# A gated MLP block: the token mix by one step of Strassen's algorithm, with its first pair of tiles inside the stage before

## The chip, the cores and the metric

The kernel runs on one core of a Trainium2 chip. A core has five engines that run side by side and meet at semaphores: TensorE (PE, matrix products; its weight loads are listed as PEld), VectorE (DVE), ScalarE (ACT), GpSimd (POOL) and SyncE (SP, which here issues transfers). Matrix products land in PSUM, a small memory of eight banks; the rest lives in SBUF, with 128 partitions. The metric is the device time of one execution in microseconds.

## What is computed

A block with adaptive layer norm: first a long convolution with gates (part A), then a gated MLP whose gate mixes the tokens (part B). The change touches part B only, with S = 2048 tokens, D = 640 and Fh = 864:

```python
h = _layernorm(x, axis=-1) * (1 + cb) + sb
z = _gelu(einsum('bsd,df->bsf', h, w_in))        # 2048 x 1728
z1 = z[..., :Fh]
z2 = _layernorm(z[..., Fh:], axis=-1)
g = einsum('ts,bsf->btf', w_sp, z2) + b_sp[None, :, None]   # the token mix
out = x + gb * einsum('bsf,fd->bsd', z1 * g, w_out)
```

The token mix multiplies a 2048 x 2048 matrix with a 2048 x 864 one. The result is bf16.

## The kernel before

Tokens are handled in 16 tiles of 128; four tiles make a group (TB = 4), so there are four groups, 0 to 3. The features of one half of z are cut into two pieces of 432 columns (FC), which fit one PSUM bank each.

**The plan.** Everything up to the normalised z2 is a list of some thousand small operations, each with an engine and its dependencies (`Plan.op`). They are issued in an order that is written out in the text `ORDER`: `P1020` means operation 1020 on PE, and A, D, G and S stand for ACT, DVE, POOL and SP. Each engine works its own operations strictly in this order.

**The z stage** (`z_group`, one call per group) is the plan's last part. For each tile, DVE adds statistics (`ln2`, L696), which are combined (L821); POOL takes the inverse root (`rstd2`, L184 and L185), DVE makes a product of it (L825), and one of DVE, ACT and POOL normalises the tile (`zx`, L835 to L839). The normalised group is transposed: group 0 on PE with its modulation on DVE and ACT (L850, L861, L863), in two halves of two tiles (`hfl`, `hmod`); groups 1 to 3 by a DMA transpose on SP (`turn`, L881), after which five modulations (`hmod2`, L887 and L889) follow on DVE, ACT or POOL. Then PE makes 16 products per group (`zz`, issued through a helper at L237), each with five matmuls of 432 columns: eight for the second half of z (which becomes z2) and eight for the first half (z1). ACT applies gelu to each (L912). For z2, DVE then takes statistics (`stz`, L918), combines them (L922), POOL and DVE make scale and shift (`rstdz`, `nmrz`), and DVE or ACT normalises z2 in place (`zn`, L933 and L935). The products go through four PSUM banks, two with the tag `pu` and two with `pz`; a product needs a bank that an earlier gelu has read. Some extra matmuls (`fill`) keep PE busy in an earlier stage.

**The token mix** follows the plan, in plain program order (the functions below). At its start SP loads transposed tiles of w_sp by DMA transpose (`load_w`, five ahead, L967) and w_o (seven DMAs). For each token tile t, `mix(t)` runs, for each of two column pieces, 16 matmuls (L974) over all token tiles of z2 in one PSUM bank, and DVE adds the bias and multiplies by z1 (L977) into the buffer u. A DMA transpose on SP turns u into uT (L980); the last tile is turned by PE and ACT (`turn_last`, L986 and L987). Two tiles later `project(t)` runs two times seven matmuls with w_o (L995), DVE adds x (L997), and the tile is written out. At t = 1 DVE multiplies w_o by the gate gb (seven products, L1013).

Memory: the tiles of part A live in pools that are closed when the plan has run; w_sp, w_o, u and uT come to lie where they were.

Of the kernel before, what the change touches and what calls it, by code (L numbers as in the profile page):

```python
# [69 lines left out]
D729 D759 P735 P749 P589 A590 D758 D731 D732 G692 D690 G760 D761 D691 A762 G763 P1036 P1037 P764 D736 D733 P765 D771  # L70
D766 D767 D768 D734 D772 P742 G667 D693 D750 G773 D774 G775 D737 D740 D739 G610 D741 D738 D694 A769 S756 A770 P787
D637 P784 D696 A788 A776 S757 D695 D836 P818 G669 P791 A785 A792 P777 D835 D837 P778 D834 A782 A819 D779 D643 D780
D781 P816 A817 G838 D839 D840 D841 A783 P794 A795 P814 P820 A842 A821 D843 S844 G848 D697 D699 G845 A815 D702 D751
D753 D701 D712 D743 D700 D698 D744 D748 D903 P798 A799 P812 A813 P826 A827 D747 P805 A806 P808 P801 A809 P822 D703
D752 D642 D849 D754 A846 A847 D704 A802 P824 A825 P886 A823 D640 A887 P850 A851 D706 P853 D611 G644 A854 D641 P857
D745 A858 P884 D900 P874 D902 A885 D746 D901 G904 D905 A875 D906 D755 D909 D907 D800 P890 A891 P880 A881 P882 P892
G908 S910 A893 A883 D876 D705 P888 A889 G912 A911 P860 P871 D810 A872 D803 D646 D807 D967 P878 A861 A913 P864 D647
A865 P867 A879 A868 D915 D914 P958 D648 D969 P923 P916 A924 A917 P946 D786 A959 P944 D645 A947 D966 D968 G970 D971
D972 G973 D796 P937 D804 A938 D975 D789 D790 A945 P933 A934 P926 D793 D797 P930 A931 G974 S976 A981 D859 D869 D866
D870 A927 D811 G828 P954 A955 D918 P952 A953 P948 G978 D932 D935 D936 A979 P940 A941 P919 D939 A949 D829 A830 D873  # L80
D877 D942 D943 D928 G980 G977 P1020 A920 A1021 P982 A983 D925 D929 D921 A833 D852 D862 D863 P996 D855 D856 G894 D895
P1024 A1025 A997 D998 D922 P989 A990 D831 P992 D899 A993 P1006 A1007 P1003 D1008 P985 A1004 D991 A986 P1014 A1015 G960
D961 P956 A957 P999 P950 A1000 A832 D896 A951 P1010 A1011 D1005 D994 P1016 A1017 D898 D987 D984 D1001 D988 D1002 D995
P1022 D1009 G1026 D1027 A964 D1029 A1031 A965 P1012 D962 D1028 D897 P1018 A1019 A1023 A1013 D1030 D963
# [3 lines left out]
class Plan:  # L88


    def __init__(self):
        self.ops, self.touch = [], {}
# [19 lines left out]
    def run(self, engines):  # L112
        order = [(x[0], int(x[1:])) for x in ORDER.split()]
        assert sorted(i for _, i in order) == list(range(len(self.ops)))
        done = set()
        for e, i in order:
            o = self.ops[i]
            assert e in o["eng"] and done.issuperset(o["deps"]), (e, i)
            o["fn"](engines[e])
            done.add(i)  # L120
# [3 lines left out]
def kernel(  # L124
# [79 lines left out]
    with ExitStack() as actx:  # L204
# [21 lines left out]
        psA = actx.enter_context(tc.tile_pool(name="psA", bufs=1, space=bass.MemoryType.PSUM))  # L226
# [713 lines left out]
        for i, k in enumerate(FILLS):  # L940
# [4 lines left out]
            op("P", "fill", fill, r=["ident"], w=["fill%d" % i], new=[("fill%d" % i, "s1")], n=k)  # L945
        plan.run({"P": nc.tensor, "A": nc.scalar, "D": nc.vector, "G": nc.gpsimd, "S": nc.sync})


    wsp_pool = ctx.enter_context(tc.tile_pool(name="wsp", bufs=1, reuse_waits="tile"))
    bwork = ctx.enter_context(tc.tile_pool(name="bwork", bufs=2, reuse_waits="tile"))  # L950
    psB = ctx.enter_context(tc.tile_pool(name="psB", bufs=2, space=bass.MemoryType.PSUM, reuse_waits="tile"))
    WB = 6
    UB = 3
    FP = NFT * P
    bsp = wsp_pool.tile([P, NT], BF16)
    nc.sync.dma_start(bsp[:], B_b_sp.rearrange("(n p) -> p n", p=P))
    bcol = wsp_pool.tile([P, NT], F32)
    nc.vector.tensor_copy(bcol[:], bsp[:])
    us = []
    for i in range(UB):  # L960
        us.append(wsp_pool.tile([P, FP], BF16, name="u%d" % i))
        nc.vector.memset(us[i][:, Fh:], 0.0)
    wTs, uTs = {}, {}

    def load_w(t):
        wTs[t] = bwork.tile([P, NT, P], BF16, tag="wT", bufs=WB, name="wT")
        nc.sync.dma_start_transpose(wTs[t][:], B_w_sp[t * P:(t + 1) * P, :])  # L967

    def mix(t):
        u = us[t % UB]  # L970
        for fc in range(NFC):
            ps = psB.tile([P, 512], F32, tag="mm", bufs=4, name="ps")
            for s_ in range(NT):
                nc.tensor.matmul(ps[:, :FC], lhsT=wTs[t][:, s_, :], rhs=tl["z2_%d" % (s_ // TB)][:, s_ % TB, fc * FC:(fc + 1) * FC],  # L974
                                 start=(s_ == 0), stop=(s_ == NT - 1))
            sl = slice(fc * FC, (fc + 1) * FC)
            nc.vector.scalar_tensor_tensor(u[:, sl], ps[:, :FC], bcol[:, t:t + 1], z1[t][:, sl], op0=ALU.add, op1=ALU.mult)  # L977
        uTs[t] = bwork.tile([P, NFT, P], BF16, tag="uT", bufs=UB, name="uT")
        if t < NT - 1:
            nc.sync.dma_start_transpose(uTs[t][:], u[:])  # L980
# [21 lines left out]

    for t in range(WB - 1):
        load_w(t)
# [45 lines left out]
```

## Time and profile before

| | |
|---|---|
| time, median of three runs | 319.19 us (318.41 to 320.23) |
| profiled execution, span from first to last instruction | 317.8 us |
| PE clock granted | 1.00 |
| first matmul of the z stage | 131.1 us |
| first matmul of the token mix | 190.1 us |
| last matmul | 315 us |

The page of a profile gives each engine's busy time and its share of the span. Below, a line of a group reads: source line, engine, operation, output<-input with the forms, count, then busy time and the mean of one in ns, then the idle time of the engine just before these instructions and who ended it. A line of the chain gives start, length and the engine's work; the chain goes back from the last instruction, at each step to what released it. A line by stretch gives for each engine the busy time and the number of instructions, then the granted clock, the DMA share and GB/s. The profiled execution has no other time of its own than its span; the runs' median lies 1.4 us above it.

### The profile page before, as it was taken

To read this page: it belongs to the slowest core of one execution; us is meant where nothing else is said; L and a number is where in the kernel's file an instruction comes from. 1 tells how busy PE (TensorE), PEld (TensorE's weight loads), DVE (VectorE), ACT (ScalarE), POOL (GpSimd) and SP (SyncE) were. 2 spreads that over 40 slices of the span, in tenths; PEclk is the share of its full clock that TensorE was granted. 3 is DMA by queue.
4 is the path that set the end of the run, shared out by engine and by line. 5 is a ranking of instruction groups with operands and counts; after the bars stand their busy time and mean duration, and the time that the engine had idled before them with its cause. 6 is when DMAs were issued, how large, how long until landed. Compare 5 with 4: busy or idle time off the path is not lost.

```text
span 317.8 us, 6393 instructions
## 1 busy us (share of the span) xinstructions
PE 306.4 (96%) x2570; PEld 203.8 (64%) x2577; DVE 205.3 (65%) x436; ACT 153.0 (48%) x273; POOL 113.2 (36%) x146
## 2 busy tenths in 40 slices
PE   7988989999999999999999999999999999999996
PEld 2665678769899988555555555555555555555554
DVE  8989989979999998898874871522222233332333
ACT  6989799978888766587667782000000000000001
POOL 2533887848897987735143310000000000000000
PEclk9999999999999999999999999999999999999999
DMA  8999999996977399030439950676556555522221
GB/s 177 246 217 253 265 251 214 217 227 171 223 205 146 103 193 324 2 71 15 82 59 166 183 148 18 131 157 113 121 116 118 116 118 116 116 52 50 50 52 62
DMA packets 127026, 45.00 MB, mean 142 GB/s; under 512 B 116144, under 2 KB 126229, under 8 KB 126997
## 3 DMA queue, kind: packets, MB, share of 16 engines
q1 hardware_dynamic: 126842, 44.55, 64.8%
q8 instruction: 20, 0.33, 0.4%
q14 instruction: 10, 0.07, 0.1%
q10 hardware_dynamic: 154, 0.05, 0.1%
HBM read 16.11 MB, written 5.24 MB: 67 GB/s over the span
## 4 chain that ended last, share of the span: by engine, by line
PE 61%; DVE 2%; ACT 1%; issue 1%; POOL 0%; DVEq 0%
PE ps L974 29%; PE pz L237 10%; PE pu L237 10%; PE po L995 10%; DVE Tf L454 1%; DVE T L454 1%; PE sm L237 1%; PE s L237 1%; ACT X L240 0%; PE pu L713 0%; POOL W L468 0%; PE s L850 0%; DVE ot L997 0%; ACT Z L240 0%; ACT KH L240 0%
## 5 line engine op out<-in xcount | busy, mean ns | idle before, releaser
L974 PE MATMUL ps<-X,wT 128*128 128x432 bf16 x512 | 95.7, 346 | 0.0
L974 PEld LDWEIGHTS <-wT 128*128 128x128 bf16 x512 | 50.1, 98 | 42.2
L987 ACT COPY uT<-pt 128x896 bf16<-128x896 bf16 x1 | 0.9, 906 | 118.5 <-PE pt L986 118.5
L237 PEld LDWEIGHTS <-Z 128*128 128x128 bf16 x320 | 31.1, 98 | 26.8 <-DVE Z L863 0.2
L237 PE MATMUL pu<-X,M 128*128 128x128 bf16 (+1 forms) x480 | 45.8, 237 | 2.2 <-DVE Tf L454 1.9
L237 PEld LDWEIGHTS <-M 128*128 128x128 bf16 x480 | 37.4, 98 | 8.8 <-issue 3.1
L977 DVE SCALAR_TENSOR_TENSOR u<-ps,bcol,G 128x432 bf16<-128x432 f32 x18 | 12.0, 668 | 42.2 <-PE ps L974 42.2
L468 POOL TENSOR_TENSOR W<-Tf 128x256 bf16<-128x256 f32 x47 | 34.7, 760 | 11.3 <-DVE Tf L454 8.0
L995 PE MATMUL po<-w_o,uT 128*128 128x320 bf16 (+2 forms) x231 | 33.2, 295 | 0.1
L237 PE MATMUL pu<-big,Z 128*128 128x432 bf16 x160 | 32.6, 346 | 0.0
L240 ACT CAST X<-s 128x1024 bf16<-128x1024 f32 x31 | 31.9, 1028 | 1.4 <-PE s L237 1.1
L237 PE MATMUL pz<-big,Z 128*128 128x432 bf16 x160 | 32.5, 346 | 0.0
L454 DVE TENSOR_TENSOR Tf<-pu,KH 128x1024 f32<-128x1024 f32 x25 | 30.3, 1219 | 2.8 <-PE pu L237 1.7
L977 DVE SCALAR_TENSOR_TENSOR u<-ps,bcol,M 128x432 bf16<-128x432 f32 x14 | 9.3, 667 | 29.9 <-PE ps L974 29.9
L995 PEld LDWEIGHTS <-uT 128*128 128x128 bf16 (+1 forms) x231 | 22.2, 98 | 9.9 <-issue 0.2
L237 PEld LDWEIGHTS <-G 128*128 128x128 bf16 x330 | 24.6, 98 | 2.0 <-issue 0.2
L240 ACT CAST KH<-pu 128x512 bf16<-128x512 f32 x40 | 22.9, 600 | 5.9 <-PE pu L237 5.9
L240 ACT CAST Z<-pz 128x512 bf16<-128x512 f32 x38 | 22.3, 601 | 5.3 <-PE pz L237 5.1
L997 DVE TENSOR_TENSOR ot<-po,xt 128x320 bf16<-128x320 f32 (+1 forms) x33 | 15.9, 482 | 12.6 <-PE po L995 12.6
L237 PEld LDWEIGHTS <-X 128*128 128x128 bf16 x288 | 17.9, 97 | 6.2 <-DMA X<-kv_scr 1.7
L918 DVE BATCH_NORM_STATS2 stz<-X 128x6 f32<-128x432 bf16 x32 | 18.0, 589 | 4.9 <-ACT X L912 4.8
L237 PE MATMUL sm<-big,dg 128*128 128x512 bf16 (+3 forms) x73 | 19.8, 379 | 0.4
(154 smaller groups left out, 421.2 us busy)
## 6 DMA issues: line engine op xcount, KB each, us to landing
wm<-in_w_mod_dram SPq DMA_DIRECT2D x6, 800.0 KB, 6.3
xt<-in_A_q_dram SPq DMA_DIRECT2D x4, 640.0 KB, 6.3
out_dram<-ot SPq DMA_DIRECT2D x15, 160.0 KB, 2.3
big<-in_B_w_in_dram SPq DMA_DIRECT2D x2, 1080.0 KB, 9.4
X<-in_A_ssm_k_dram SPq DMA_DIRECT2D x4, 512.0 KB, 5.2
kv_scr<-big SPq DMA_DIRECT2D x4, 512.0 KB, 4.0
X<-kv_scr SPq DMA_DIRECT2D x4, 512.0 KB, 4.6
w_o<-in_B_w_out_dram SPq DMA_DIRECT2D x6, 160.0 KB, 3.0
```

The source lines that it names most:

```text
L237: nc.tensor.matmul(o, lhsT=w, rhs=x, start=start, stop=stop)
L240: (e.copy if e is nc.scalar else e.tensor_copy)(dst, src)
L454: e.tensor_tensor(T_[:], (tl[pu] if src is None else tl[src])[:, :, :, None, :].to_broadcast(shape), tl[KH][:, :, None, :, :].to_broadcast ...
L468: e.tensor_tensor(tl[W][:, :, o, :], T_[:, :, 0, o, :], T_[:, :, 1, 1 - o, :], op=ALU.add if o else ALU.subtract)
L918: op("D", "stz", lambda e, i=i, n=n, fc=fc: e.bn_stats(out=stz[:, n, fc, :], in_=tl[z2][:, i, fc * FC:(fc + 1) * FC]), r=[(z2, (i, fc))], ...
L974: nc.tensor.matmul(ps[:, :FC], lhsT=wTs[t][:, s_, :], rhs=tl["z2_%d" % (s_ // TB)][:, s_ % TB, fc * FC:(fc + 1) * FC], start=(s_ == 0), st ...
L977: nc.vector.scalar_tensor_tensor(u[:, sl], ps[:, :FC], bcol[:, t:t + 1], z1[t][:, sl], op0=ALU.add, op1=ALU.mult)
L987: nc.scalar.copy(uTs[t][:], pt[:])
L995: nc.tensor.matmul(ps[:, :hi - lo], lhsT=uTs[t][:fsz[ft], ft, :], rhs=w_o[:fsz[ft], ft, lo:hi], start=(ft == 0), stop=(ft == NFT - 1))
L997: nc.vector.tensor_tensor(ot[:, lo:hi], ps[:, :hi - lo], xt[:, t, lo:hi], op=ALU.add)
```

## The change

The mix matrix A (w_sp) is cut into two by two blocks of 1024 tokens, and B (z2) into two by two blocks of 1024 tokens and 432 columns. One step of Strassen's algorithm in Winograd's form gives the four blocks of the result from seven block products in place of eight, with sums of blocks ahead and behind. Tile p of the upper token half and tile p + 8 of the lower one are worked as a pair, eight pairs in all, and a product is eight matmuls of 432 columns:

- `s_sum`: for each pair, DVE makes four sums S1 to S4 of w_sp's blocks, each 128 x 1024 bf16.
- `t_sum`: once, DVE makes the sums T1 to T4 of z2's blocks, in eight pieces of 128 x 1728 bf16; T3 is written over the upper right block of z2.
- `product(p, m)`: products 1, 5, 6 and 7 begin in a new PSUM bank (a, d, b and c); 2, 3 and 4 are added in PSUM to banks a, d and c.
- `keep`: ACT copies products 1 and 5 (with the bias) to SBUF as f32.
- `c11`, `partial`, `c22`, `last_sum`: DVE puts the four result blocks together with bias and z1. `turn_u` transposes u by DMA, for the last tile too; `turn_last` is gone.

The plan now has 48 more operations, for the loads of three pairs, w_o, the products of w_o with gb, S sums of pairs 0 and 1, all T sums, and the whole of pair 0. `begin_mix` closes part A's pools when the first of them is issued, so that every operation of part A stands ahead of it in the order. In `ORDER` all of the text from the z stage's start on is new. SP's order there is now: turn of group 1, w_sp tile 9, w_o, tile 1, turn of group 2, tiles 0, 8 and 10, turn of group 3, b_sp, tile 2, and the two turns of u. Most products for the second half of z in groups 2 and 3 come ahead of those for the first half; pair 0 runs as M1, a z product, M5, M6, M7, M2, M3, M4, and two z products stand behind it. Of the five modulations of group 2, POOL has four (before: one).

```diff
-        self.ops, self.touch = [], {}
+        self.ops, self.touch, self.late = [], {}, None
...
+            if self.late is not None and i >= self.late[0]:
+                self.late[1]()
+                self.late = None
...
+        def s_sum(p, k):
+            if k == 0:
+                Ss[p] = [bwork.tile([P, HT, P], BF16, tag="S%d" % i, bufs=2, name="S%d" % (i + 1)) for i in range(4)]
+            S = Ss[p]
+            x, y, o = ((a_of(p, 1, 0), a_of(p, 1, 1), ALU.add), (S[0][:], a_of(p, 0, 0), ALU.subtract),
+                       (a_of(p, 0, 0), a_of(p, 1, 0), ALU.subtract), (a_of(p, 0, 1), S[1][:], ALU.subtract))[k]
+            nc.vector.tensor_tensor(S[k][:], x, y, op=o)
...
+            nc.vector.tensor_tensor(y if o is None else T[o][:, sl, :], x, y, op=ALU.subtract)
+
+        BANK = {1: "a", 2: "a", 3: "d", 4: "c", 5: "d", 6: "b", 7: "c"}
...
+            more = m in (2, 3, 4)
+            if not more:
+                part[p, BANK[m]] = alloc(BANK[m])
+            ps = part[p, BANK[m]]
+            for s_ in range(HT):
+                nc.tensor.matmul(ps[:, :FC], lhsT=lhs[:, s_, :], rhs=rhs(s_), start=(s_ == 0 and not more), stop=(s_ == HT - 1),
+                                 skip_group_check=more)
...
+        def partial(p):
+            part[p, "s"] = f32("s1")
+            nc.vector.tensor_tensor(part[p, "s"][:], part[p, "b"][:, :FC], part[p, 1][:], op=ALU.add)
+
+        def c22(p):
+            c_ = f32("c22")
+            nc.vector.tensor_tensor(c_[:], part[p, "c"][:, :FC], part[p, "s"][:], op=ALU.add)
+            nc.vector.tensor_tensor(c_[:], c_[:], part[p, 5][:], op=ALU.add)
+            nc.vector.tensor_tensor(ubuf(p, 1)[:, FC:Fh], c_[:], z1[p + HT][:, FC:], op=ALU.mult)
+
+        def last_sum(p, bank, i, f):
+            c_, sl = f32("c"), slice(f * FC, (f + 1) * FC)
+            t = p + HT * i
+            nc.vector.scalar_tensor_tensor(c_[:], part[p, bank][:, :FC], T["bcol"][:, t:t + 1], part[p, "s"][:], op0=ALU.add, op1=ALU.add)
+            nc.vector.tensor_tensor(ubuf(p, i)[:, sl], c_[:], z1[t][:, sl], op=ALU.mult)
...
-    for t in range(NT + 2):
-        if t < NT:
-            mix(t)
...
-        if t == NT - 1:
-            turn_last(t)
+    for p in range(1, HT):
+        nxt = p + 1 < HT
+        product(p, 1, bank)
+        keep(p, 1)
+        product(p, 5, bank)
+        keep(p, 5)
+        if nxt:
+            s_sum(p + 1, 0)
+            s_sum(p + 1, 1)
+        product(p, 2, bank)
+        c11(p)
+        if nxt:
+            s_sum(p + 1, 2)
+        product(p, 6, bank)
+        partial(p)
+        product(p, 7, bank)
+        c22(p)
+        product(p, 3, bank)
+        last_sum(p, "d", 0, 1)
+        turn_u(p, 0)
+        if nxt:
+            project(p - 1)
+        product(p, 4, bank)
+        last_sum(p, "c", 1, 0)
+        if p + 3 < HT:
+            load_w(p + 3)
+            load_w(p + 3 + HT)
+        turn_u(p, 1)
+        if nxt:
+            project(p - 1 + HT)
+            s_sum(p + 1, 3)
+    for p in range(HT - 2, HT):
+        project(p)
+        project(p + HT)
```

## The prediction

> **What bounds the kernel now.** I read the page's busy shares first, then busy time by stage, then the chain of waits from the z stage on, then the groups of the engines that the change loads more, and last the timelines around the transfers that it moves.
>
> ```profile
> PE 306.4 (96%) x2570; PEld 203.8 (64%) x2577; DVE 205.3 (65%) x436; ACT 153.0 (48%) x273; POOL 113.2 (36%) x146
> ```
>
> An average says little, so by stage (the columns are PE, PEld, DVE, ACT, POOL; 132 to 196 us is the z stage, then the token mix):
>
> ```profile
> 132.00:196.00 64.00, 64.00 (x360) 34.58 (x358) 46.12 (x139) 44.22 (x80) 21.51 (x29) 1.00 0.48 90
> 196.00:316.00 120.00, 118.82 (x719) 69.38 (x717) 39.32 (x71) 0.91 (x1) 0.00 (x0) 1.00 0.46 99
> ```
>
> PE is busy throughout both, at full clock. That busy might hide gaps, since matmul ends are modelled, so I look at the chain (start, length, what):
>
> ```profile
> 189.34 0.91 PE pu L237 x5
> 190.25 17.52 PE ps L974 x96
> 207.77 1.91 PE po L995 x14
> 209.68 5.84 PE ps L974 x32
> ...
> 302.68 5.84 PE ps L974 x32
> 308.52 1.91 PE po L995 x14
> 310.82 2.88 PE po L995 x21
> ```
>
> Each piece begins where the last one ended: 32 mix matmuls in 5.84 us, so 0.1825 us each; 14 of the projection in 1.91 us; five of the z stage in 0.91. From 131 us to the end PE issues without a gap, and the mix follows the z stage at once. A matmul taken out there is worth 0.1825 us, if nothing else becomes late. The two candidates are DVE, with 46.1 of 64 us taken in the z stage, and the SP queue.
>
> [...] For bf16 the trace has 405 ns at 512 columns[...].
>
> ```profile
> L997 DVE TENSOR_TENSOR ot<-po,xt 128x320 bf16<-128x320 f32 (+1 forms) x33 | 15.9, 482 | 12.6 <-PE po L995 12.6
> L977 DVE SCALAR_TENSOR_TENSOR u<-ps,bcol,G 128x432 bf16<-128x432 f32 x18 | 12.0, 668 | 42.2 <-PE ps L974 42.2
> L653 DVE TENSOR_TENSOR gh<-gh,gsa_bf 128x512 bf16<-128x512 bf16 x1 | 0.4, 405 | 0.0
> ```
>
> **Part 1: matmuls removed.** Before: 16 blocks x 2 halves x 16 = 512. After: 8 pairs x 7 products x 8 = 448. 64 x 0.1825 = 11.68 us. turn_last goes too: seven transposes, and in the chain 310.82 - 308.52 - 1.91 = 0.39 us. Gross gain 12.07 us. Projections are unchanged (16 x 1.91).
>
> **Part 2: the pair loop (pairs 1 to 7).** PE per pair: 56 x 0.1825 + 2 x 1.91 = 14.04 us. DVE per pair: four S sums of 1024 bf16[...], 2.68; c11 0.67 (the form of L977); partial 0.61; c22 three sums of 0.607, 1.82; two last_sum of 0.667 + 0.607, 2.55; four ot adds, 1.97. Sum 10.3 us, so 3.7 us are spare[...]. ACT has two copies of some 0.55 us. Order within a pair (us from its start, 1.46 per product): M1, M5, M2, M6, M7, M3, projection at 8.76, M4 at 10.67, projection.
> - M2 adds to M1's bank and must wait for ACT's copy of it: 0.36 us after the last matmul plus 0.55, inside M5's 1.46. Hidden.
> - M4 adds to M7's bank and must wait for c22's first sum: M7 ends at 7.30, sum done by 8.3, M4 starts at 10.67. In the last pair no projection stands between: 8.3 against 8.76. Hidden.
> - S sums for the next pair run in DVE's waits; weights are loaded two pairs (28 us) ahead against 4.6 us of landing. Hidden.
> - End: uT of the last block now comes by DMA: 0.36 + 0.67 + 0.61 + 2.9 (uT<-u, issue to landing) = 4.5 us after M4, while three projections (5.7 us) run. Hidden by 1.2 us.
>
> So the loop stays on PE: no stall.
>
> **Part 3: the z stage with pair 0 in it.** Here DVE gets 7 S sums, 8 T sums of 1728 bf16[...], five of the seven w_o products, then the pair's own sums. I walked the streams in the new order with the durations of the rows. I find four places.
>
> (a) Group 0. DVE has one more L738 (0.67), a bn_stats (0.28) and an aggregate (0.12) ahead of the three modulations (L863) that release the first z matmuls, which before ended at 131.42; it had 0.33 us of idle there. Some 0.65 us late, and 0.3 for the second flips, now after two z tiles instead of four. Stall 1.0.
>
> (b) Group 2's transpose. SP's order was turn of groups 1, 2, 3, bsp, five wT, seven w_o:
>
> ```profile
> 139.22 27.21 SPq L881 DMA_TRANSPOSE Z<-Z  x3
> 166.88 0.38 SPq L956 DMA_DIRECT2D bsp<-in_B_b_sp_dram  x1
> 167.32 14.09 SPq L967 DMA_TRANSPOSE wT<-in_B_w_sp_dram  x5
> 181.45 3.42 SPq L1007 DMA_DIRECT2D w_o<-in_B_w_out_dram  x7
> ```
>
> Now one wT, w_o and a second wT go between turns 1 and 2, three wT between turns 2 and 3. With 2.2 to 2.9 us of issue for a wT and 3.4 for w_o, SP is through them at about 151 us, if their memory is free by 143 (the last residual adds in my walk). The turn itself waits for the norms of group 2, for which DVE has 20.1 us of queue behind it against 17.5 before: it goes out at 155.5 instead of 151.9 and lands 5.1 us later at 160.6. Then POOL does four of five modulations (before: one), 0.76 us each: done at 163.7. PE wants the fourth weight at 162.8. Behind the turn on SP stand three wT and turn 3; behind POOL's modulations stands group 3's rstd, for which DVE waits until about 165 (counted in c). Stall 1.0; bounds 0 (if DVE is as fast as before) and 3.0 (if SP is only let go at 147, where the old order has the last residual add).
>
> (c) The chain behind the last second half of z. After it PE has five z tiles (4.56 us), M1, another z tile and M5 before it needs T2: 8.4 us. DVE from that tile: 2.7 us of gelu, statistics and aggregates, T1's first half and a norm beside POOL's rstd (1.4), then 3 norms, T2's half, a norm, T2's half: T2 is ready 8.3 us on. By queue sums DVE has 15.0 us of work between group 3's modulation and that point, and is some 0.4 us behind. So T2 is just in time, T3 (1.96 us later) within M6's 1.46 plus what M5 lost, T4 well before M4. But M5 needs a bank whose gelu stands on ACT behind two norms (1.1 us each) of group 3: ready about 0.55 us late. Stall 0.6. Bounds 0 and 2.5, if DVE is 2 us further behind.
>
> (d) The last two z tiles, behind M4, use banks freed by c11 and partial: done 1 us earlier. The first loop product takes banks of finished fills. 0.
>
> Sum of stalls: 1.0 + 1.0 + 0.6 = 2.6 us, bounds 0 and some 6.5; below nothing is excluded, since the old chain has no PE gap here to win back. What hides c's chain is the five z tiles of first halves; without that cover (second halves last) 4.6 us more would show.
>
> **The sum.** 12.07 - 2.6 = 9.5 us off. The profiled execution has a span of 317.8, so a span of 308.3. The page gives no other time for it; the median of the runs is 1.4 us above that span, which I leave as it is: 319.19 - 9.5 = 309.7.
>
> **Rivals.**
> 1. No stalls: DVE and ACT just keep up. For: in the old z stage PE has no gap even where DVE is busy for 7.8 of 8 us (140 to 148), and group 2 had about 1 us of slack. Against: sums above. 319.2 - 12.1 = 307.1.
> 2. DVE or SP late in the z stage by all upper bounds: two or three stalls grow to 6 us together. For: DVE is 98% busy in 140 to 148 and the new sums come on top; SP stands still while it waits for memory. Against: DVE idles some 12 of the 59 us in the old z stage. 319.2 - 12.1 + 6.2 = 313.3.
> 3. Slower: DVE becomes the bound of the pair loop. A pair took 2 x (5.84 + 1.91) = 15.5 us before; with 7 pairs the 12 us are eaten when DVE needs more than 14.04 + 9.5 / 7 = 15.4 us per pair, half more than my 10.3; at 16.2 the time is 319.2 - 9.5 + 7 x 2.2 = 325. For: 19 in-order DVE instructions, each behind a PE product. [...]
> That it computes something else, or leaves matmuls in place, I don't see: seven products of eight matmuls are in the code.
>
> **How the numbers follow.** Forecast (307.6 to 312, stalls of 0.5 to 5) 55%; rival 1 20%; rival 2 18%; rival 3 5%; something within 0.5% 2%. The likeliest gives 309.7. The range reaches from rival 1 less 0.6 of spread, 306.5, to rival 2 with 0.3, 313.6; outside are rival 3 and the ends of the others. Some 0.5% (1.6 us) is what a measurement of this kernel tells from no change. Faster 0.93, same 0.02, slower 0.05.
>
> **What would show it.** The matmul count: 448 mix matmuls at 0.1825 and no group of transposes at the end. Loop: chain pieces of PE alone, a period of 14.0 us, DVE near 10.3 of 14. z stage: PE idle of about 1 us near 131 to 135, near 162, and 0.6 before M5; turn 2 issued near 155. Wrong if the loop shows PE waiting for DVE or for uT, or if the idle time before 205 is over 6 us.

## The result, and the profile after

The changed kernel takes 315.25 us (median of four runs, 315.20 to 315.81) against 318.8 us of the kernel before beside it (318.40 to 320.23): a ratio of 0.987, with a 95% interval of 0.983 to 0.991. The interval lies below 1, so it is faster, by about 4 us or 1.3%; the forecast was 9.5 us and its range ended at 313.6. The profiled execution has a span of 313.4 us, 4.4 less than before.

The busy shares of the page, then busy time by stage (z stage with pair 0, then the pair loop; the columns are PE, PEld, DVE, ACT, POOL, then clock, DMA share and GB/s):

```profile
PE 297.4 (95%) x2506; PEld 196.9 (63%) x2506; DVE 252.9 (81%) x513; ACT 159.9 (51%) x286; POOL 122.7 (39%) x152
```

```profile
132.00:208.00 76.00, 71.74 (x402) 37.34 (x399) 64.37 (x167) 43.97 (x81) 30.96 (x35) 1.00 0.41 84
208.00:312.00 104.00, 102.20 (x622) 60.22 (x620) 69.34 (x124) 8.74 (x16) 0.00 (x0) 1.00 0.52 111
```

PE has lost its full row in the first line: 71.7 of 76 us. The chain of waits shows the loop (start, length, what):

```profile
207.77 8.76 PE ps L1013 x48
216.53 1.91 PE po L1137 x14
218.43 1.46 PE ps L1013 x8
219.90 1.91 PE po L1137 x14
221.81 8.76 PE ps L1013 x48
230.57 1.91 PE po L1137 x14
```

From 207.77 to 221.81 is one pair, 14.04 us, each piece beginning where the last one ended. The loop does what the change meant. The same chain ahead of it is no longer PE's alone. It goes through DVE, POOL, a transfer and ACT:

```profile
139.66 1.03 POOL rstd L191
...
142.21 5.79 DMA Z<-Z
...
148.09 0.81 ACT Z L895
148.90 0.84 ACT X L920 x2
...
162.12 3.58 POOL Z L897 x4
...
165.78 0.21 POOL rstd L190
...
166.06 1.02 POOL rstd L191
...
167.11 0.16 DVE nmr L833
...
194.45 2.11 ACT X L941 x2
196.56 0.42 ACT G L920
```

PE's timeline names the waits. Each line is start, length, what, and in brackets the idle time ahead of it and who ended it:

```profile
149.79 1.17 PE L245 MATMUL pu<-big,Z 128*128 128x432 bf16 x5 [1.30 <-ACT X L920]
...
197.02 1.62 PE L1013 MATMUL pz<-T,S 128*128 128x432 bf16 x8 [1.75 <-ACT G L920]
```

The brackets are a little short, since a matmul's end is modelled. So I add up lost time from starts: the start of the next piece, less the start of this one, less 0.1825 us for each matmul of 432 columns (0.056 for one of 128) in it. From the first z matmul to the start of the loop the kernel before loses 0.0 us by this sum, and the changed one loses:

| place | lost, us | forecast, us |
|---|---|---|
| group 0 and its second flips | 0.80 | 1.0 |
| group 1, first product | 1.56 | 0 |
| group 2 | 0.73 | 1.0 |
| group 3 | 1.06 | 0 |
| ahead of M5 | 1.91 | 0.6 |
| all | 6.05 | 2.6 |

Three more terms close the balance. One is a wait of about 0.4 us in the tail. The second is 1.04 us in part A, which the change leaves alone: PE's last block of work ahead of the z stage starts at 131.37 us against 130.33. Of this, 0.84 us is there at the first product after the scratch tile kv_scr has come back (23.79 against 22.95). Over the profiles of this study the first z matmul came between 130.0 and 133.1 us, in the old and the new order alike. The third is 0.20 us between that last block and the first z matmul (132.37 against 131.13 in all). There the new order has begun, and PE's weight loads wait for DVE's modulation of group 0. So: 12.07 - 6.05 - 0.4 - 1.04 - 0.20 = 4.4 us, which is the difference of the spans.

### The profile page after: what moved, and what is told of

It is laid out like the page before. It is cut to its first block, busy times and chain, and to the rows that moved or that the text cites. A ratio compares the mean times of both kernels' runs of the same rounds, so it can differ in the third digit from the quotient of the medians.

```text
span 313.4 us, 6409 instructions
## 1 busy us (share of the span) xinstructions
PE 297.4 (95%) x2506; PEld 196.9 (63%) x2506; DVE 252.9 (81%) x513; ACT 159.9 (51%) x286; POOL 122.7 (39%) x152
## 4 chain that ended last, share of the span: by engine, by line
PE 38%; DVE 10%; POOL 5%; DMA 2%; ACT 1%; issue 1%; POOLq 0%; DVEq 0%; ACTq 0%
PE ps L1013 22%; PE po L1137 9%; DVE stz L926 3%; PE pu L245 3%; PE pz L1013 2%; DMA Z<-Z 2%; PE pz L245 2%; DVE S L988 1%; POOL rstdz L191 1%; POOL Z L897 1%; PE pu L1013 1%; DVE st L704 1%; POOL Z L845 1%; ACT X L941 1%; POOL rstd L191 1%
## 5 line engine op out<-in xcount | busy, mean ns | idle before, releaser
L245 PE MATMUL pu<-X,M 128*128 128x128 bf16 (+1 forms) x480 | 45.8, 237 | 2.2 <-DVE Tf L462 1.9
L1019 ACT COPY m<-ps 128x432 f32<-128x432 f32 x7 | 3.6, 519 | 72.3 <-PE ps L1013 72.3
L1013 PEld LDWEIGHTS <-S 128*128 128x128 bf16 x256 | 25.0, 98 | 23.6 <-issue 2.0
L245 PE MATMUL pz<-big,Z 128*128 128x432 bf16 x160 | 33.5, 346 | 0.8 <-POOL Z L897 0.8
L1013 PEld LDWEIGHTS <-wT 128*128 128x128 bf16 x192 | 18.7, 98 | 15.2
L1013 PE MATMUL ps<-X,wT 128*128 128x432 bf16 x112 | 22.7, 346 | 0.0
L1013 PE MATMUL ps<-T,S 128*128 128x432 bf16 x112 | 22.7, 346 | 0.0
L1013 PE MATMUL ps<-X,S 128*128 128x432 bf16 x112 | 21.6, 346 | 0.0
L245 PE MATMUL s<-F1bd,X 128*128 128x256 bf16 x128 | 19.2, 272 | 2.0 <-DVE X L400 1.6
L245 PE MATMUL sm<-big,dg 128*128 128x512 bf16 (+1 forms) x80 | 20.4, 379 | 0.0
```

The source lines that it names most:

```text
L245: nc.tensor.matmul(o, lhsT=w, rhs=x, start=start, stop=stop)
L1013: nc.tensor.matmul(ps[:, :FC], lhsT=lhs[:, s_, :], rhs=rhs(s_), start=(s_ == 0 and not more), stop=(s_ == HT - 1), skip_group_check=more)
L1019: nc.scalar.copy(part[p, m][:], part[p, BANK[m]][:, :FC])
```

## The experiments

Each run stands beside the kernel before on its own chip, at 319.3 to 320.6 us in median. Because part A varies by up to 3 us, stalls are compared by the lost time between the first z matmul and the pair loop. The intervals of many rows overlap, so the times alone don't tell rows apart that lie within some 2 us of each other.

| run | time, us | ratio, 95% interval | group 0 | group 1 | group 2 | group 3 | pair 0 | lost, all |
|---|---|---|---|---|---|---|---|---|
| changed kernel | 315.25 | 0.983 to 0.991 | 0.8 | 1.6 | 0.7 | 1.1 | 1.9 | 6.05 |
| new order alone | 322.33 | 1.006 to 1.010 | 0.8 | 1.3 | 0.2 | 0 | 0.7 | 2.89 |
| sums left out | 310.38 | 0.964 to 0.977 | 0.8 | 1.5 | 0.8 | 0.5 | 0 | 3.59 |
| old order, sums set in | 308.29 | 0.959 to 0.968 | 0 | 0 | 0 | 0 | 0.4 | 0.44 |
| old order, sums behind | 314.43 | 0.981 to 0.988 | 0 | 0 | 0 | 0 | 3.9 | 3.88 |
| modulations spread | 313.57 | 0.973 to 0.985 | 0.8 | 1.5 | 1.3 | 0 | 1.4 | 4.96 |
| gelu first | 314.65 | 0.980 to 0.987 | 0.8 | 1.5 | 0.7 | 1.1 | 1.6 | 5.63 |
| T1 apart | 314.30 | 0.981 to 0.987 | 0.8 | 1.6 | 0.8 | 1.1 | 1.9 | 6.15 |
| residuals moved | 315.72 | 0.985 to 0.990 | 0.4 | 2.6 | 1.9 | 1.0 | 1.9 | 7.85 |
| residuals, modulations, gelu | 314.31 | 0.981 to 0.985 | 0.4 | 2.6 | 1.3 | 0 | 1.2 | 5.48 |

For the second row "pair 0" is a wait ahead of the last z product, for a bank. The last columns are all from one profiled execution each. Where runs share the order of a stretch they repeat well: the changed kernel and the runs "gelu first" and "T1 apart" agree within about 0.1 us in each of the four groups.

**The new order without Strassen's step.** The kernel before, mix and all, with its z stage in the order of the change. The order says which engine does an operation too: 26 old operations are on another engine in the change.

```diff
-ORDER (the text of the kernel before)
+ORDER (the text of the change, operations 0 to 1037 only)
```

> The kernel before, with the new order for its own operations in the z stage; the token mix as it was, no block sums. Theory (the rewritten order itself brings the idle time of PE in groups 0 to 2, about 3.3 us in the profile after): PE idles about 0.9 us at group 0, 1.5 us where group 1 begins and 0.8 us at group 2, and the time is 2.5 to 4 us above before, 321.3 to 322.8. Rival (the order is neutral, DVE's added sums bring the idle time): within 1 us of before, no PE gap where group 1 begins.

322.33 us: slower than before by 0.6 to 1.0%, and 2.89 us lost where the old order loses none. Almost half of the stalls are there with no sum, no load of weights and no pair 0 in the stage. Groups 0 and 1 came about as expected; group 2 did not, with 0.2 us in place of 0.8.

**The sums left out.** Neither T sums nor the S sums of pairs 0 and 1 are made; the products read blocks of w_sp and z2 as they are.

```diff
         def s_sum(p, k):
+            if p < 2:
+                return
...
         def t_sum(k, h):
+            return
```

> The kernel after with the T sums and the S sums of pairs 0 and 1 left out: the products of these pairs read blocks of w_sp and z2 that were not summed. Theory (two causes): the gaps at groups 0 and 1 (2.4 us) and at group 2 (0.8) stay, those at group 3 and before M5 (2.8 us) go; time 2.5 to 3.5 us below after, near 312.3. If the sums were the whole cause all of 6.5 us would go, 308.7; if only the order, the time stays at 315.

310.38 us with 3.59 us lost. That is 4.9 us less time, but only 2.5 us less lost; in the profile the rest lies in part A, where the first z matmul came at 130.0. The gap ahead of M5 is gone and that of group 3 shrinks to 0.5 us; those of groups 0 to 2 stay. So the order makes the gaps of groups 0 and 1, and the sums on DVE the one ahead of M5. The two between have more than one cause. Group 3's gap is not there with the order alone and is half gone without the sums. Group 2's needs no sums, and the order alone leaves only 0.2 us of it. The order alone also lacks the loads of w_sp and w_o on SP and the products of w_o on DVE. With the loads group 2's transpose landed 5.3 us after its issue (5.4 in this run), without them after 4.9. That fits, but no run takes the loads alone away.

**Old order, with the sums set into DVE's pauses.** Nothing is left out: w_o comes ahead of the transpose of group 2, three w_sp tiles ahead of that of group 3, the S sums of pair 0 and one product of w_o where DVE stood still for 3.4 us (from 166.5 us of the kernel before), and pair 0 behind the last z product, as M1, M5, M2, M6, M7, M3, M4. One norm of group 3 goes from ACT to DVE, and on ACT one gelu comes ahead of a norm of group 2; every other old operation has the engine that it had before. DVE's timeline of the kernel before shows the pause, in brackets:

```profile
169.86 1.12 DVE L918 BATCH_NORM_STATS2 stz<-X 128x6 f32<-128x432 bf16 x2 [3.40 <-ACT X L912]
```

The edit, in words:

```diff
-SP   turn1 wT9 w_o wT1 turn2 wT0 wT8 wT10 turn3 bsp wT2
+SP   turn1 w_o turn2 wT0 wT8 wT1 turn3 wT9 bsp wT2 wT10
-P    M1, a z product, M5 M6 M7 M2 M3 M4, two z products
+P    M1 M5 M2 M6 M7 M3 M4, no z product left
```

> The kernel after, but the z stage in the order of the kernel before, with the new operations set into DVE's and SP's idle stretches of that profile and pair 0 behind the last z product (M1, M5, M2, M6, M7, M3, M4). Theory (the gain went to the order, the sums fit into DVE's idle time): no PE gap before M1, under 1.5 us from M1 to the pair loop, the loop's period 14.05 us; time 10 to 11.5 us below before, 307.5 to 309. Rival (DVE has too much to do in the z stage in any order): gaps of 4 us or more, 312 or above.

308.29 us, a ratio of 0.963: better than both kernels (95% interval 0.959 to 0.968). The timeline of PE in pair 0 shows the one wait of the z stage and pair 0:

```profile
189.83 1.62 PE L1015 MATMUL pu<-X,wT 128*128 128x432 bf16 x8
191.29 1.62 PE L1015 MATMUL pz<-T,S 128*128 128x432 bf16 x8
192.75 1.62 PE L1015 MATMUL pu<-X,wT 128*128 128x432 bf16 x8
194.21 1.62 PE L1015 MATMUL pu<-T,S 128*128 128x432 bf16 x8
195.67 3.08 PE L1015 MATMUL pz<-X,S 128*128 128x432 bf16 x16
199.03 1.62 PE L1015 MATMUL pz<-T,wT 128*128 128x432 bf16 x8 [0.28 <-DVE c L1041]
```

M4 waits 0.28 us for the first sum of c22; everything else follows at once. The same sums and products come with 0.44 us lost here and about 6 us in the order of the change.

**Old order, the new operations all behind it.** What the placing is worth.

```diff
+ORDER: the old text, then loads, S of pair 0, T, pair 0, S of pair 1, products of w_o
```

> The changed kernel with the order of the kernel before for the z stage, and all new operations (loads of w_sp and w_o, sums S and T, pair 0, the products of w_o with gb) behind it in plain program order, none planned into the z stage. Nothing is left out. Theory (the gross gain of 12 us is whole, the reordered z stage costs 3 us and the sums in it another 3): no gap ahead of M1, so the 3 us of the order are won back, but the sums T are now in the open: M5 to M2 wait some 3.5 us for them, and 2 to 4 us more go to the sums S of pair 1 and the products of w_o that stand in DVE's queue ahead of pair 0's bank sums; 312 to 314. Rival (the sums fit anywhere, since DVE idles in the mix): below 310. Rival (the sums cost as much in the open as in the z stage and there is nothing in the placing): over 315.

314.43 us. The lost 3.88 us are the waits ahead of M1 (1.45, for a bank whose gelu stands on ACT behind three norms), M5 (1.15 and 0.24 within it, for T1) and M4 (1.05). In pair 1, 1.89 us more go ahead of M5 to an S sum still to be made, and 0.61 ahead of a projection. That the sums "fit anywhere" is refuted; setting them in, with the gelu and the norm moved as in the run before, is worth some 6 us.

**Group 2's modulations spread again.** Two on ACT, two on DVE, one on POOL, in place of four on POOL.

```diff
-G911 G913 G914 (three modulations of group 2 on POOL)
+A911 A913 D914
```

> The kernel after, but group 2's modulations as before: two on ACT, two on DVE, one on POOL (in place of four on POOL and one on DVE), each put where the transpose is due. Theory (POOL's four modulations hold up group 3's inverse root, for which DVE's queue and with it the chain to M5 waits): the gap at group 2 (0.7 us) goes, group 3's statistics come 2 us earlier, and 1 to 2.5 us are gained, 312.8 to 314.3. Rival (DVE is behind for its own load): at most 0.7 us gained, 314.6 or above.

313.57 us, 4.96 us lost. The gap of group 3 is gone: with POOL free, the inverse root for group 3 no longer stands behind four modulations. But the gap of group 2 grows from 0.7 to 1.3, since ACT's modulations come late.

**The gelu ahead of two norms.** One ACT instruction moved.

```diff
-A1029 A1031 A1025 (two norms of group 3, gelu)
+A1025 A1029 A1031
```

> The changed kernel with one ACT instruction moved: the gelu that frees M5's bank stands ahead of the two group-3 norms on ACT that it stood behind. Nothing is left out. Theory (DVE's chain of norms and the T2 sum is as late as the bank): the gap of 1.75 us before M5 goes, but M6 then waits for T2, whose last piece ended at about 198.3 against M6's start at 198.48, and the two norms on ACT are some 1.3 us later, so T3 and T4 too; gain at most 0.3 us, about 315. Rival (the prediction's step: the bank alone is the bound there): M5 and all behind it come 1.5 us or more earlier, about 313.7, and there is no new gap before M6 or M2.

314.65 us. The gap of 1.91 ahead of M5 goes, and 0.87 ahead of M6, 0.26 within M6, 0.25 ahead of M7 and 0.22 within M7 come: 0.3 us better in pair 0. M6 first waits for a bank, whose gelu stands behind the same norms, and not for T2 as I had said; its second half then waits for the second half of T2, which DVE ended at 198.17, 0.05 us ahead of it. M7 waits for T3. Bank, T2 and T3 are about equally late, so freeing the one bank is worth next to nothing.

**T1 away from POOL's inverse root.** Two DVE instructions moved.

```diff
-D  T1 first half, statistics, nmrz of group 2 ... T1 second half, norm, nmrz of group 3
+D  nmrz of group 2, T1 first half ... norm, nmrz of group 3, norm, T1 second half
```

> The changed kernel with the two T1 pieces moved on DVE, behind the scale-and-shift product of group 2 and behind the first norm of group 3, so that neither runs while POOL takes the inverse root of z2's variance. Nothing is left out. Theory (POOL's small instructions are slowed by a DVE sum of bf16 that runs beside them): POOL's two instructions take 0.2 and 1.0 us again in both groups, against 0.9 to 1.9 us; group 3's scale and shift are ready some 0.8 us earlier, the gap before M5 shrinks by 0.5 to 1 us, about 314.4. Rival (POOL is slow for another reason, or the time is DVE's queue anyway): POOL's durations stay, or they fall and the gap before M5 stays at 1.7 us; 315.2.

POOL's timeline in the changed kernel, then in this run (four of its inverse-root instructions for z2, for groups 2 and 3):

```profile
187.42 0.19 POOL L190 TENSOR_SCALAR rstdz<-mvz 128x4 f32<-128x4 f32 x1 [5.49 <-DVE mvz L930]
187.70 1.93 POOL L191 TENSOR_TENSOR rstdz<-rstdz,mhalf 128x4 f32<-128x4 f32 x1
192.05 0.89 POOL L190 TENSOR_SCALAR rstdz<-mvz 128x4 f32<-128x4 f32 x1 [2.42 <-DVE mvz L930]
193.01 1.14 POOL L191 TENSOR_TENSOR rstdz<-rstdz,mhalf 128x4 f32<-128x4 f32 x1
```

```profile
185.56 0.20 POOL L192 TENSOR_SCALAR rstdz<-mvz 128x4 f32<-128x4 f32 x1 [5.49 <-DVE mvz L932]
185.84 1.01 POOL L193 TENSOR_TENSOR rstdz<-rstdz,mhalf 128x4 f32<-128x4 f32 x1
190.24 0.33 POOL L192 TENSOR_SCALAR rstdz<-mvz 128x4 f32<-128x4 f32 x1 [3.39 <-DVE mvz L932]
190.65 1.01 POOL L193 TENSOR_TENSOR rstdz<-rstdz,mhalf 128x4 f32<-128x4 f32 x1
```

The slowing is real: 4.15 us for the four instructions with T1 beside them, 2.55 without. The time is not won: 1.28 us lost ahead of M5 in place of 1.91, but 0.18 within M6 and 0.25 and 0.22 at M7. What came behind on DVE was about as late as POOL.

**The beginning in the old order.** Four runs put whole beginnings of the z stage back. The first two take group 2's transpose with them, although the expectation says "up to the transposes of group 1"; so on SP one wT, w_o and another wT came behind it. The other two end at group 1's transpose. The second and the fourth also have the modulations spread and the gelu first.

```diff
-ORDER from the z stage's start: the text of the change
+ORDER from the z stage's start to turn2 (later turn1): the old text; what is left, in the change's order
```

> The changed kernel with the beginning of the z stage (up to the transposes of group 1, all engines) in the order of the kernel before, the rest as the change has it. Nothing is left out. Theory (the gaps at group 0 and group 1, about 1.0 and 1.5 us, come from the new order of norms and statistics there, and the gaps behind are made by orders of their own): those two gaps go and the others stay, 2 to 2.5 us less, 312.7 to 313.3. Rival (DVE's queue over the whole z stage is the bound, and the early gaps only lie where its debt is paid): the gaps at the start go but those at group 2, group 3 and in pair 0 grow by as much, over 314.5.

> As the run before, and besides with group 2's five modulations on ACT twice, DVE twice and POOL once, and with the gelu that frees M5's bank ahead of the two norms of group 3 on ACT. Nothing is left out. Theory (the stalls add up, each with a cause of its own): 2.3 us for the beginning, 1.1 for the modulations and 0.4 for the gelu as each gave alone, 3.8 together, about 311.4, still some 3 us above the old order with the sums set into it. Rival (one queue is behind all of them): no better than the beginning alone.

> The changed kernel with the beginning of the z stage up to group 1's DMA transpose, on all engines, in the order of the kernel before, and the rest, all of SP's loads too, as the change has it. (The run with the longer beginning took group 2's transpose into it as well, so one w_sp tile, w_o and another w_sp tile came behind that transpose on SP.) Nothing is left out. Theory (the gaps at group 0 and 1, 1.0 and 1.5 us, are made by the order of norms and statistics there): both go, and PE's start of the pair loop is 2 to 2.5 us earlier counted from the first z matmul; about 313. Rival (DVE owes the work anyway, and the statistics and residual additions that now come behind the transpose make group 2 later): the gaps at groups 2 and 3 grow by as much, over 314.5.

> As the run before, and besides with group 2's five modulations on ACT twice, DVE twice and POOL once, and with the gelu that frees M5's bank ahead of the two norms of group 3 on ACT. Nothing is left out. Theory (the stalls add up): the beginning's gain, 1.1 us for the modulations and 0.4 for the gelu, together 3.5 to 4, about 311.5, still some 3 us above the old order with the sums set into it. Rival (one queue is behind all): no better than the run before within 0.5 us.

317.53, 318.34, 317.76 and 315.49 us, with 9.61, 9.57, 8.66 and 7.18 us lost. In the first two the gaps of groups 0 and 1 are gone, as the theory said: PE loses nothing in the first 30 us of the stage. But no time is won by it, for each run brought a new fault. In the first two SP was busy until 171.7 and 170.8 us with wT, w_o and four more wT, and the transpose of group 3 went out 40.7 and 40.3 us after the first z matmul, against 37.3 with the change. In the other two, four residual additions on POOL came to lie beside DVE's norms for group 1. DVE's timeline, then POOL's, of the third run:

```profile
139.86 1.11 DVE L835 SCALAR_TENSOR_TENSOR nmr<-mv,rstd 128x4 f32<-128x4 f32 x1 [0.41 <-POOL rstd L193]
140.89 3.75 DVE L849 TENSOR_SCALAR Z<-xt,mv,rstd 128x640 bf16<-128x640 bf16 x3
```

```profile
139.80 4.66 POOL L700 TENSOR_TENSOR xt<-xt,gh 128x512 bf16<-128x512 bf16 x4
```

Three norms take 3.75 us on DVE while POOL adds; in the kernel before they take 1.16:

```profile
137.98 1.16 DVE L839 TENSOR_SCALAR Z<-xt,mv,rstd 128x640 bf16<-128x640 bf16 x3
```

Group 1's transpose left 11.6 us after the first z matmul, against 9.8 with the change. And after pauses of 2.51 and 0.39 us PE's granted clock was 0.71 from 152 to 154 us and 0.50 from 154 to 156. The other three profiles have such a stretch too, behind pauses of 4.63 us (first run), of 0.41, 0.58 and 0.68 (second), and of 2.60 and 0.39 (fourth): there nine to fifteen matmuls of 432 columns stand 0.29 to 0.36 us apart in place of 0.1825, and in the first the clock was 0.56 and 0.59 in the two stretches of 2 us from 178 to 182 us. The mean clock of the four profiled executions is 0.993 or 0.994. So a part of the lost time of all four is clock. Modulations and gelu together took 2.3 us off the third run (317.76 to 315.49), and nothing off the first.

**Group 1 by itself.** Work of later groups moved out of the way of group 1's norms, with SP, ACT and PE in the order of the change. D750 and D743 are products, D751 a residual addition, D712 a gate and D752 statistics of later groups; G611, G702 and G697 are residual additions of later groups on POOL. First these and two more were moved; then POOL's residual addition for group 1 (G667) was also put where the kernel before has it, which is the diff shown.

```diff
-G763 G611 G773 G776 G667 G669 G702 G838 G841 G697 G644
+G763 G667 G773 G776 G669 G838 G841 G697 G611 G702 G644
-D750 D772 D733 D771 D766 D767 D768 D751 D774 D637 D712 D752 ... D743 D839 D840 D843
+D772 D733 D771 D766 D767 D768 D750 D774 D637 ... D839 D840 D843 D751 D712 D752 D743
```

> The changed kernel with ten instructions moved in the first 12 us of the z stage and nothing else (SP, ACT and PE keep their order): on DVE the product, the residual addition and the statistics that belong to later groups come behind the modulations of group 0 or behind the norms of group 1, and on POOL two residual additions come behind group 1's norm, none of them beside DVE's norms. Nothing is left out. Theory (the gaps at group 0 and group 1 come from work of later groups that the new order puts ahead of their norms): turn of group 1 goes out 9.8 us or less after the first z matmul becomes possible, the gap at group 1 shrinks from 1.5 to 0.5 us or less, group 0's by some 0.5, and the time is about 313.8; up to 0.5 of it comes back at group 2. Rival (DVE's debt only moves): group 2's and group 3's gaps grow by as much as is won, 315 or more.

> As the run before, and besides with group 2's five modulations on ACT twice, DVE twice and POOL once, and with the gelu that frees M5's bank ahead of the two norms of group 3 on ACT. Nothing is left out. Theory (the stalls add up, each of its own cause): 1.5 us for the beginning, 1.1 for the modulations, 0.4 for the gelu, 312.2. Rival (one queue, DVE's, is behind all): within 0.5 us of the run before.

> As the run that moved ten instructions (only six of them now on DVE and POOL kept, and group 0's order of statistics left as the change has it), and besides POOL makes group 1's residual addition ahead of the inverse root of group 0's second pair, where the kernel before has it, instead of behind the norm that follows. Nothing is left out. Theory (that addition, 1 us late on POOL, is what holds DVE's statistics of group 1: DVE stood 1.02 us for it once its own queue was cleared): DVE no longer waits there, group 1's transpose goes out 9 us or less after the first z matmul (10.7 in that run, 9.84 with the change), the gap at group 1 falls from 1.8 to 0.5 us or less, and the pair loop starts 1.5 us or more earlier, counted from the first z matmul, than with the change; about 314. Rival (the gap at group 1 is bound by the landing of the transpose or by DVE's queue as a whole): the gap stays over 1 us.

> As the run before, and besides with group 2's five modulations on ACT twice, DVE twice and POOL once, and with the gelu that frees M5's bank ahead of the two norms of group 3 on ACT. Nothing is left out. Theory (the stalls add up): a further 1.5 us for modulations and gelu, 312.5. Rival: within 0.5 us of the run before.

The first two, without and with modulations and gelu, gave 316.67 and 315.52 us, with 9.17 and 7.52 us lost: with DVE's queue cleared, DVE stood 1.02 us for G667, which in the change comes behind a norm on POOL. With that mended (315.72 us) group 1's transpose leaves 8.6 us after the first z matmul in place of 9.8, and its result is there at 144.6. Yet PE waits as before, now for DVE. Timelines of ACT, DVE and PE in that run:

```profile
144.60 0.81 ACT L897 ACTIVATE Z<-Z,sb_col,cb_col 128x512 bf16<-128x512 bf16 x1 [0.97 <-DMA Z<-Z]
```

```profile
147.91 0.72 DVE L899 TENSOR_SCALAR Z<-Z,cb_col,sb_col 128x512 bf16<-128x512 bf16 x2
```

```profile
148.36 0.68 PE L247 MATMUL pu<-big,Z 128*128 128x432 bf16 x2 [1.10 <-DVE Z L899]
```

ACT modulates as soon as the transfer has landed, DVE 3.3 us later: two modulations stand behind statistics, which the moved work has pushed back. A second wait, of 1.18 us for a bank, comes later in the group. So group 1 loses 2.6 us in place of 1.6, and group 2 1.9 in place of 0.7. The rival holds: the debt of DVE's queue is only paid elsewhere. With modulations and gelu added (314.31 us) 2.4 us of the lost time go and 1.4 us of the time. Singly they took off 1.1 and 0.4 us of lost time, so these two do add up; the beginning stays as bad.

**One bank more for the projection.** The old order with the sums set in, with one PSUM bank given from the products to the projection.

```diff
-        return psB.tile([P, 512], F32, tag="mm", bufs=6, name="ps")
+        return psB.tile([P, 512], F32, tag="mm", bufs=5, name="ps")
-            ps = psB.tile([P, 512], F32, tag="o", bufs=2, name="po")
+            ps = psB.tile([P, 512], F32, tag="o", bufs=3, name="po")
```

> The version with the z stage's old order and the new operations set into the idle stretches of DVE and SP (308.3 us when it ran), with one PSUM bank more for the projection and one fewer for the products in the last stage, so that projection 6 need not wait for the additions behind the last sum. Nothing is left out. Theory: the gap of 0.3 to 0.4 us before projection 6 goes, 307.9. Rival: the products now lack a bank and PE waits once per pair, 7 waits of 0.3 us or more, over 309.

310.5 us (ratio 0.967 to 0.975): worse than with six banks, by about 1.1 us in the profiles from the first z matmul to the end; the rest of the 2.2 us between the medians is not explained. The wait of about 0.4 us ahead of projection 6 is gone, as the theory said, but pair 1's M5 now waits 1.85 us for a bank that DVE's last sum of pair 0 frees; later pairs do not wait. The rival is right in kind, once and not seven times. The version of 308.29 us stands as the best.

## Why the prediction was wrong

**Right: the gross gain and the loop.** 12.07 us of matmuls and transposes went. The period is 14.04 us as computed. The groups of DVE in the loop (line, operation, forms, count, then busy time and mean in ns, idle before) bear the prices out. A sum of f32 took 608 ns, also with an operand in PSUM, against 607 in the forecast; a straight line through two rows of the kernel before (324 ns for 160 columns, 492 for 320, operand in PSUM) gives 610 as an estimate. No row of the kernel before shows the price of the S sums, 2.68 us for four; four took 2.74 (681 to 692 ns each):

```profile
L1046 DVE SCALAR_TENSOR_TENSOR c<-ps,bcol,s 128x432 f32<-128x432 f32 x14 | 9.3, 664 | 5.2 <-PE ps L1013 5.1
L988 DVE TENSOR_TENSOR S<-wT 128x1024 bf16<-128x1024 bf16 x13 | 8.9, 682 | 0.0
...
L1039 DVE TENSOR_TENSOR c<-ps,s 128x432 f32<-128x432 f32 x7 | 4.3, 608 | 5.5 <-PE ps L1013 5.5
```

T sums took 1.00 to 1.06 us each, the two of T3 2.02 together (1.96 in the walk of (c), which no row of the kernel before shows either). Rival 3, DVE as the bound of the loop, is out. (It counts 19 DVE instructions per pair; there are 17.)

**Wrong: the term "sum of stalls, 2.6 us".** It measured 6.05 us, so the prediction's own sign of being wrong, over 6 us of idle time before 205, came true. The step that failed is the walk of the streams behind this term: it has nothing for group 1, it ends the delay of (b) at group 2, and it makes (c) too small. By its parts:
- (a) group 0, 1.0: 0.80 behind the first z matmul and 0.20 ahead of it. Right in size, not in place: the forecast had some 0.65 ahead of it.
- Not named at all: group 1, 1.56 us. The prediction has no term for it and no reason for leaving it out. But in the new order its statistics, a residual addition on POOL and its norms come later, and the transpose leaves 9.8 us after the first z matmul (before: 8.1, from 139.22 and 131.13). The run of the order alone has the same 9.8 us, and 1.3 us lost there.
- (b) group 2, 1.0: 0.73. Right. But I let the delay end there. POOL's four modulations hold the inverse root for group 3, DVE stands 3.3 us for it (I had counted to 165; it came at 167.1, of which 1.2 us is the later start of the whole stage), and group 3 loses 1.06 us. Spreading the modulations removed that gap. They do not make it alone: the run of the order alone has the same four on POOL and no gap there.
- (c) ahead of M5, 0.6: 1.91. The bank was the late part, as said; its gelu stood behind norms that waited for DVE and POOL, which were later than the walk had them. Without the sums the gap is not there. That the bank alone decides is refuted by the run with the gelu first.
- (d) 0: right. The tail, "hidden by 1.2 us", cost about 0.4, and not for the transfer that the forecast priced: the projection waits for additions that stand in DVE's queue behind the last sums.

The bounds that I gave, 0 and 6.5, held the measured sum, and so did rival 2 with its 6 us; but I set the likeliest value too near the low end and gave this rival 18%. Its 313.3 us plus the tail and the late start (1.24 us) comes to 314.9, close to what was measured.

**The common cause.** In the z stage DVE has work for most of the time and takes it strictly in order: in the profile of the changed kernel its 513 instructions start in the order of the program, but for one clearing of a buffer that is listed 0.01 us out of place. The prediction's first reading had it less full: it took 132 to 196 us as the z stage, with DVE busy for 46.1 of 64 us, but that takes in 6 us of the mix. To 190 us it is 45.8 of 59 in the kernel before:

```profile
131.00:190.00 59.00, 59.00 (x342) 31.94 (x339) 45.84 (x138) 42.49 (x79) 21.54 (x29) 1.00 0.52 98
```

In the change DVE stands for POOL's inverse root of the group norms 5.5 us in all (before 3.5, and 3.0 in the old order with the sums set in). The list of waits of the changed kernel's DVE in that stage (who waits for whom, us in total, times, longest):

```profile
DVE nmr L833 <- POOL rstd L191: 5.5, 3, 3.3
```

Behind the longest of these waits, from 163.8 to 167.1, stood a product of w_o, whose loads SP had issued by 151.5; it started at 168.06. (SP stands in the same way until a buffer is free: in the pair loop its loads of w_sp waited ten times for PE, 17.9 us in all.) That work was ready behind the others too is not shown. The old order has the same work in another sequence, and partly on other engines, and loses 0.44 us. So neither the amount of work nor the algorithm is at fault, but the order. What is not settled is which smallest set of moves would mend the order of the change itself; the moves that mended the beginning only moved the wait. How much of groups 2 and 3 is due to the loads is open too.

## What to carry to other kernels

When a change brings a new sequence for in-order engines, price the sequence apart from the new work: the old order with the new work set into its pauses was 7 us faster here than the order that was rewritten around it. A delay that is found at one group must be walked on to the next group and to the buffer behind it. How full a queue is does not tell whether it will be late: DVE worked 64.4 of 76 us in the changed kernel, with 6.05 us lost, and 63.4 of 70 us (from 131 to 201 us) in the old order with the sums set in, with 0.44 lost. And before a stall is repaired, ask which second chain is about as late, since taking away one of two gives nothing.

## What was not expected of the hardware

- DVE and POOL slowed each other. POOL's inverse root took 1.93 us in place of 1.01 beside a T sum, and three norms on DVE took 3.75 us in place of 1.16 beside POOL's additions. The walk had left most of it out. What decides who is slowed does not show: POOL's instruction of 1.93 us is listed 0.02 us ahead of the T sum (187.70 against 187.72), and yet it was the one to take longer; that T sum took 1.04 us, within the 1.00 to 1.06 of the others.
- PE's granted clock fell to about half after short pauses in some executions, and in others it did not. With 0.49 and 1.32 us of idle within 2.5 us (the run of ten moved instructions) the clock was 0.62 and 0.52 in the two stretches of 2 us from 150 to 154 us, and 1.7 us more were lost, nearly as much as the pauses took. In the changed kernel the pause of 1.3 us ahead of 149.8 brought no fall (1.00 from 148 to 156 us). Nor did pauses of 0.44 and 1.37 us, at the same place in the same moves with modulations and gelu (1.00 from 152 to 156 us). And of the 18 executions of the run of ten, four, the profiled one among them, show a mean clock of 0.994 or 0.995, and the others 0.998 or more. What tells the two outcomes apart is open. Busy time by stretch in the run of ten, then behind the like pauses in the other (columns as above, the clock third from the end):

```profile
150.00:152.00 2.00, 2.00 (x7) 0.85 (x8) 2.00 (x6) 0.53 (x1) 0.00 (x0) 0.62 0.88 268
152.00:154.00 2.00, 2.00 (x7) 0.87 (x6) 1.97 (x9) 0.00 (x0) 0.00 (x0) 0.52 0.92 205
```

```profile
152.00:154.00 2.00, 1.98 (x10) 0.99 (x11) 2.00 (x6) 0.53 (x1) 0.00 (x0) 1.00 0.97 264
154.00:156.00 2.00, 2.00 (x12) 1.08 (x11) 1.97 (x9) 1.43 (x3) 0.00 (x0) 1.00 1.04 198
```
